# The last first-layer group accumulates onto a seed in PSUM, the second of seven products moves up, and the planner prices array-mode changes anew

## The chip, the cores and the metric

The kernel runs on one core of a Trainium2 chip. The metric is the device time of one execution in microseconds (us), the median of several runs. Engines are named as in the profile: PE (TensorE, the matrix engine), DVE (VectorE), ACT (ScalarE), POOL (GpSimd) and SP (SyncE, which here issues all DMAs).

## What is computed

Banded attention over 2 x 8 heads of 768 tokens, then two MLPs on the 1536 tokens of width 512:

```python
x = attention(q, k, v)                       # local band of 96 and 8 global keys, linear bias
h = np.maximum(x @ w_in, 0.0)                # w_in 512 x 2048
y = h * h @ w_out                            # w_out 2048 x 512: the "first layer" here
xn = y / np.sqrt(mean(y * y) + 1e-6) * rms_g
g = xn @ w_gate; val = xn @ w_val            # 512 x 1536 each: the "gated layer"
out = (g * sigmoid(g) * val) @ w_out2
```

All of it is in fp32. Each fp32 operand of the MLPs is split into a high and a low part, and a matmul becomes three: high x high, high x low, low x high (lines 334, 335, 336). Such three matmuls of 384 columns are called a triple below.

## The kernel before

Nothing is issued in the order of the source. Every operation is recorded with its engine, a modelled duration, its reads and writes and a due time; `Plan.solve` then runs a list scheduler over the model: the engine that is free first takes, of its ready operations, the one due first. Due times come from the operations that need a result, and for a triple from a running clock in the order in which the source records it. The order found is issued, and each engine executes its own list strictly in that order; a wait in the model is not a wait on the chip, and the reverse. Operations on PE have a mode: "row" (scores, line 824), "col" (probabilities times v, line 861) or "full" (all else), since they split the array differently. The model adds `MODE` = 0.095 us whenever the mode changes, and stays in the present mode if an operation of it is due within 0.25 us. While PE would idle in the first 30 us, dummy matmuls ("fillers", line 1124) are put in.

The tokens are 4 chunks (c = 0 to 3) of 384. The stages, by the time of the trace:

- Attention, 0 to 165 us: 48 tiles, chunk by chunk, each a chain of scores on PE, maximum on DVE, exponential on ACT, scaling on DVE, transposes on PE, copy on ACT and product with v on PE. Triples of the first layer for finished chunks fill PE in between.
- First layer, to 387 us: `first(g, c)` for groups g = 0 to 3 of 4 x 128 hidden columns. Its first half multiplies x by w_in into banks b4, b7, b5, b6 (groups 1 to 3); `relu2` has ACT read each bank (line 435), square it twice (436, 437) and DVE form the low part (438). Its second half multiplies the hidden values by w_out into b0 to b3, one bank for each of 4 output blocks e; group 0 copies the banks into the tile y on ACT (line 466), the later groups add them to y on DVE (line 469).
- Norm: during group 3, `norm_sum` squares y on ACT (481, 486), adds on DVE (487), sums over partitions on PE (489), takes the root on ACT (492) and the reciprocal on DVE in three pieces (495). `norm(p)`, for the pair p of chunks (2p, 2p + 1), forms the normed blocks and their differences on DVE (516, 521), the high parts on ACT and the low parts on DVE (both `split`, lines 324 and 325; results in the x tiles, or in ar).
- Gated layer, 378 to 678 us: w_gate and w_val are applied to pairs of chunks by a scheme of seven products instead of eight (`PRODUCTS`). A `quad` is one such set, six for gate and six for value per pair, each product two triples. Banks are (b1, b2, b3) = (4, 5, 6) for gate and (7, 2, 3) for value. Product 1 goes to b1 and is copied by ACT into b2 (line 551), where 6, 7 and 4 accumulate; 5 goes to b3 and ACT copies it out (554); DVE adds b2 to it after product 6 (557) and 7 (565); 2 accumulates on b1; 3 on b3. `sink` is what consumes an output. `final` multiplies by w_out2 (512 columns, lines 608 and 611).

Of the kernel before, what the change touches and what calls it, by code (L numbers as in the profile page):

```python
# [24 lines left out]
KD = DM // P  # L25
CH = 384
# [10 lines left out]
G1 = 4  # L37
N1 = FF1 // P // G1
# [12 lines left out]
QHI = KHI = "ACT"  # L51
EPS = "POOL"
NSLACK = 0.5


def f32(ap):
# [11 lines left out]
class Plan:  # L68
# [1 line left out]

    MODE = 0.095

    def __init__(self):
        self.ops = []
# [26 lines left out]
    def solve(self):  # L103
        for o in reversed(self.ops):
            for q in o.succ:
                o.due = min(o.due, q.due - o.dur - (o.lat if q.eng != o.eng else 0.0))
        engines = sorted({o.eng for o in self.ops})
        free = dict.fromkeys(engines, 0.0)
        mode = dict.fromkeys(engines)
        wait, ready = {e: [] for e in engines}, {e: [] for e in engines}  # L110
        for o in self.ops:
            o.left, o.ready = len(o.deps), 0.0
            if not o.left:
                heappush(wait[o.eng], (0.0, o.n, o))
        self.fill, done, filling, held = [], 0, True, 0.0
        while done < len(self.ops):
            best = None
            for e in engines:
                if ready[e]:
                    t = free[e]  # L120
                elif wait[e]:
                    t = max(free[e], wait[e][0][0])
                else:
                    continue
                if best is None or t < best[0]:
                    best = (t, e)
            t, e = best
            while wait[e] and wait[e][0][0] <= t:
                o = heappop(wait[e])[2]
                heappush(ready[e], (o.due, o.n, o))  # L130
            if held > t + 0.05 and any(not x[2].port for x in ready[e]):
                o = min(x for x in ready[e] if not x[2].port)[2]
                ready[e].remove((o.due, o.n, o))
                ready[e].sort()
            else:
                o = heappop(ready[e])[2]
            if o.port:
                t = max(t, held)
            if o.mode != mode[e] and len(ready[e]) and o.mode:
                other = [x for x in ready[e] if x[2].mode == mode[e] and x[0] < o.due + 0.25]  # L140
                if other:
                    heappush(ready[e], (o.due, o.n, o))
                    o = min(other)[2]
                    ready[e].remove((o.due, o.n, o))
                    ready[e].sort()
            if o is self.last_fill:
                filling = False
            if e == "PE" and t < FILL and filling:
                x = max(free[e] + 0.1, 5.0)
                while x + 0.3 < t:  # L150
                    self.fill.append(x)
                    x += 0.3
            extra = self.MODE if o.mode and mode[e] and o.mode != mode[e] else 0.0
            if o.mode:
                mode[e] = o.mode
            o.start = t
            o.end = t + o.dur + extra
            free[e] = o.end
            if o.port:
                held = o.end  # L160
            done += 1
            for q in o.succ:
                q.ready = max(q.ready, o.end + (o.lat if q.eng != e else 0.0))
                q.left -= 1
                if not q.left:
                    heappush(wait[q.eng], (q.ready + q.slack, q.n, q))
        return self
# [12 lines left out]
ACT = lambda n: 0.07 + n / 1200  # L180
# [37 lines left out]
class Mlp:  # L218
# [109 lines left out]
    def mm3(self, bank, w, a, first, last, width, rs, due=None):  # L328
        nc = self.nc

        def go():
            ps = self.tl(f"b{bank}")[:, :width]
            (wh, wl), (ah, al) = w(), a()
            nc.tensor.matmul(ps, lhsT=wh, rhs=ah, start=first, stop=False, skip_group_check=True)  # L334
            nc.tensor.matmul(ps, lhsT=wh, rhs=al, start=False, stop=False, skip_group_check=True)  # L335
            nc.tensor.matmul(ps, lhsT=wl, rhs=ah, start=False, stop=last, skip_group_check=True)  # L336
        dur = 3 * (0.0125 + width * 0.41797e-3)
        if due is None:
            due = self.clock
            self.clock += dur  # L340
        return self.op("PE", dur, go, rs, [("b", bank)], due=due, mode="full")
# [99 lines left out]
    def first(self, g, c, banks, dues=None, k_major=False):  # L441

        nc = self.nc
        b1, b2 = banks
        acts = [self.act() for _ in range(G1)]
        order = [(k, f) for f in range(G1) for k in range(KD)]
        if k_major:
            order = [(k, f) for k in range(KD) for f in range(G1 - 1)] + [(k, G1 - 1) for k in range(KD)]
        due = lambda: dues.pop(0) if dues else None
        for k, f in order:  # L450
            w, rw = self.w[("in", g * G1 + f), k]
            mm = self.mm3(b1[f], w, lambda k=k: self.x(k, c * CH, c * CH + CH), k == 0, k == KD - 1, CH,
                          rw + self.both(self.xres(k, c * CH, c * CH + CH)), due())
            if g == 0 and c == 0 and f == G1 - 1 and k == 0:
                self.plan.last_fill = mm
            if k == KD - 1:
                self.relu2(lambda f=f: self.tl(f"b{b1[f]}")[:, :CH], [("b", b1[f])], acts[f])
        order = [(e, f) for e in (0, 1) for f in range(G1 - 1)] + [(0, G1 - 1), (1, G1 - 1)]
        order += [(e, f) for e in range(2, KD) for f in range(G1)]
        for e, f in order:  # L460
            w, rw = self.w[("out", g * G1 + f), e]
            self.mm3(b2[e], w, acts[f][0], f == 0, f == G1 - 1, CH, rw + self.both(acts[f][1]), due())
            if f == G1 - 1:
                ps = lambda e=e: self.tl(f"b{b2[e]}")[:, :CH]
                if g == 0:
                    self.op("ACT", ACT(CH), lambda e=e, ps=ps: nc.scalar.copy(self.y(e, c), ps()),
                            [("b", b2[e])], self.yres(e, c))
                else:
                    self.op("DVE", DVE(CH), lambda e=e, ps=ps: nc.vector.tensor_tensor(
                        out=self.y(e, c), in0=ps(), in1=self.y(e, c), op=ALU.add),  # L470
                        [("b", b2[e])] + self.yres(e, c), self.yres(e, c))
# [3 lines left out]
    def norm_sum(self, c, bank):  # L475
# [3 lines left out]
        for e in range(KD):  # L479
# [10 lines left out]
            ps(), lhsT=self.ones, rhs=s(), start=True, stop=True, skip_group_check=True), rs, [("b", bank)],  # L490
            due=self.clock - (12.0 if bank == 7 else 0.0), mode="full", slack=NSLACK)
        self.op("ACT", ACT(CH) + 1.3, lambda: nc.scalar.activation(
# [48 lines left out]
    def quad(self, key, p, banks, sink):  # L541

        nc, tl = self.nc, self.tl
        b1, b2, b3 = banks
        ps = {b: (lambda b=b: tl(f"b{b}")[:, :CH]) for b in banks}
        n = self.np5 % 2
        self.np5 += 1
        p5, r5 = (lambda: tl(f"p5{n}")), [("p5", n)]
        rb = lambda b: [("b", b)]
        self.product(1, b1, key, p, True)  # L550
        self.op("ACT", ACT(CH), lambda: nc.scalar.copy(ps[b2](), ps[b1]()), rb(b1), rb(b2))
        yield
        self.product(5, b3, key, p, True)
        self.op("ACT", ACT(CH), lambda: nc.scalar.copy(p5(), ps[b3]()), rb(b3), r5)
        yield
        self.product(6, b2, key, p, False)
        self.op("DVE", DVE(CH), lambda: nc.vector.tensor_tensor(  # L557
            out=ps[b3](), in0=ps[b2](), in1=p5(), op=ALU.add), rb(b2) + r5, rb(b3))
        yield
        self.product(2, b1, key, p, False)  # L560
        sink(0, 0, ps[b1], rb(b1))
        yield
        self.product(7, b2, key, p, False)
        t, rt = self.ra(5)
        self.op("DVE", DVE(CH), lambda: nc.vector.tensor_tensor(
            out=t(), in0=ps[b2](), in1=p5(), op=ALU.add), rb(b2) + r5, rt)
        sink(1, 1, t, rt)
        yield
        self.product(3, b3, key, p, False)
        sink(0, 1, ps[b3], rb(b3))  # L570
        yield
        self.product(4, b2, key, p, False)
        sink(1, 0, ps[b2], rb(b2))
        yield
# [626 lines left out]
```

## Time and profile before

| | us |
|---|---|
| median of 3 runs (lowest to highest) | 676.8 (674.68 to 677.08) |
| the profiled execution, its own time | 680.09 |
| its span, first to last instruction | 678.3 |
| PE busy in the span | 653.2 |
| DVE busy | 496.6 |
| ACT busy | 387.6 |
| POOL busy | 152.2 |

The profiled execution is 3.3 us longer than the median; all times of the trace below are of it. Busy times are of matmuls whose ends are modelled and overlap, so PE at full share tells that it never waited, and not that each matmul was as short as it can be.

### The profile page before, as it was taken

What the parts mean: (1) busy time and instruction counts of PE and PEld (TensorE: products, weight loads), DVE (VectorE), ACT (ScalarE), POOL (GpSimd) and SP (SyncE); (2) the same over time, 40 slices, a digit from 0 to 9 for tenths busy, and PEclk for the clock granted to TensorE, in tenths of its full rate; (3) what the DMA queues carried; (4) which work ended last, traced back from release to release, by engine and by line L of the source; (5) the groups of instructions that cost most, each with busy time, mean ns of one, the idle gap of its engine ahead of it and who ended that gap; (6) DMA issues with size and microseconds to landing.
All of it is one profiled execution on the core that took longest, in us unless ns stands there. A gap on an engine that the chain in (4) does not pass through costs nothing. (4 is left out here: it accounts for less than half of the span.)

```text
span 678.3 us, 10579 instructions
## 1 busy us (share of the span) xinstructions
PE 653.2 (96%) x3823; PEld 592.3 (87%) x3823; DVE 496.6 (73%) x1098; ACT 387.6 (57%) x865; POOL 152.2 (22%) x187
## 2 busy tenths in 40 slices
PE   5998999998999999999999979999999999999996
PEld 4676877777999999999999968999999999998994
DVE  6989987673888966226768998877876987777434
ACT  5789878785765664346666775654353444443310
POOL 1100010002232321005300111544144234442000
PEclk9789999998999999999999988999999999999999
DMA  5435542210233323002210000131111210310022
GB/s 201 158 111 186 168 146 93 77 47 1 94 125 104 114 94 125 0 1 63 66 59 1 32 31 1 62 125 64 63 62 63 94 63 32 125 63 0 2 81 110
DMA packets 18158, 52.69 MB, mean 78 GB/s; under 512 B 2608, under 2 KB 3888, under 8 KB 18096
## 3 DMA queue, kind: packets, MB, share of 16 engines
q1 hardware_dynamic: 18096, 51.92, 23.3%
q8 instruction: 32, 0.52, 0.3%
q14 instruction: 30, 0.25, 0.1%
HBM read 48.76 MB, written 3.15 MB: 77 GB/s over the span
## 5 line engine op out<-in xcount | busy, mean ns | idle before, releaser
L325 POOL TENSOR_TENSOR M<-wbits,M 128x512 fp32r<-128x512 f32 x60 | 83.0, 1387 | 246.3 <-ACT M L324 194.6
L334 PE MATMUL b<-xh,M 128*128 128x384 f32 x336 | 117.1, 349 | 4.5 <-ACT xh L324 2.8
L335 PE MATMUL b<-xl,M 128*128 128x384 f32 x336 | 114.0, 339 | 2.0 <-DVE xl L325 2.0
L336 PE MATMUL b<-xh,M 128*128 128x384 f32 x336 | 113.8, 339 | 0.0
L438 DVE TENSOR_TENSOR h<-ra,h 128x384 fp32r<-128x384 f32 x64 | 37.3, 586 | 49.0 <-ACT ra L437 49.0
L334 PEld LDWEIGHTS b<-xh,M 128*128 128x128 f32 x336 | 64.1, 191 | 10.1 <-ACT xh L324 3.6
L335 PEld LDWEIGHTS b<-xl,M 128*128 128x128 f32 x336 | 64.0, 191 | 4.2 <-DVE xl L325 2.6
L336 PEld LDWEIGHTS b<-xh,M 128*128 128x128 f32 x336 | 63.9, 190 | 0.0
L324 ACT CAST M<-wbits 128x512 fp32r<-128x512 f32 x68 | 41.8, 617 | 37.0 <-DVE wbits L374 10.7
L334 PE MATMUL b<-h,M 128*128 128x384 f32 x176 | 61.6, 350 | 0.0
L611 DVE TENSOR_TENSOR y<-b,y 128x512 f32<-128x512 f32 x60 | 41.1, 688 | 26.2 <-PE b L336 25.8
L335 PE MATMUL b<-h,M 128*128 128x384 f32 x176 | 59.0, 335 | 0.7 <-DVE h L438 0.7
L336 PE MATMUL b<-h,M 128*128 128x384 f32 x176 | 59.0, 335 | 0.0
L435 ACT ACTIVATE ra<-b 128x384 f32<-128x384 f32 x64 | 31.2, 487 | 47.5 <-PE b L336 47.2
L366 ACT ACTIVATE wbits<-wraw 128x512 f32<-128x512 f32 x68 | 45.2, 668 | 20.7 <-DMA wraw<-in_w_in_dram 8.0
L336 PE MATMUL b<-M,h 128*128 128x512 f32 x144 | 56.9, 395 | 0.0
L335 PE MATMUL b<-M,h 128*128 128x512 f32 x144 | 56.6, 393 | 0.0
L334 PE MATMUL b<-M,h 128*128 128x512 f32 x144 | 56.2, 390 | 0.1
L371 DVE SCALAR_TENSOR_TENSOR wbits<-wraw,wbits 128x512 int32<-128x512 int32 x68 | 55.1, 811 | 1.5
L835 ACT ACTIVATE p<-p,mn 128x256 f32<-128x256 f32 (+1 forms) x96 | 46.5, 486 | 13.2 <-DVE mn L831 11.2
L374 DVE SCALAR_TENSOR_TENSOR wbits<-wraw,wbits 128x512 int32<-128x512 int32 x68 | 48.4, 714 | 0.9
L839 POOL TENSOR_SCALAR rs<-sm 128x2 f32<-128x2 f32 x48 | 12.7, 265 | 143.4 <-ACT p L835 143.4
(124 smaller groups left out, 1598.6 us busy)
## 6 DMA issues: line engine op xcount, KB each, us to landing
wraw<-in_w_out_dram SPq DMA_DIRECT2D x28, 512.0 KB, 3.5
wraw<-in_w_in_dram SPq DMA_DIRECT2D x16, 512.0 KB, 3.5
wraw<-in_w_gate_dram SPq DMA_DIRECT2D x12, 512.0 KB, 3.5
wraw<-in_w_val_dram SPq DMA_DIRECT2D x12, 512.0 KB, 3.5
raw<-in_kq_dram SPq DMA_DIRECT2D x8, 480.0 KB, 3.5
v<-in_vab_dram SPq DMA_DIRECT2D x8, 384.0 KB, 3.0
out_dram<-y SPq DMA_DIRECT2D x12, 256.0 KB, 2.1
raw<-in_kq_dram SPq DMA_DIRECT2D x7, 416.0 KB, 3.4
```

Of the source, the lines that this page charges most:

```text
L324: self.op("ACT", ACT(n), lambda: nc.scalar.copy(dst()[0], src()), rs, [(x, "hi") for x in ws])
L325: self.op(eng, t(n), lambda: e.tensor_tensor(out=dst()[1], in0=src(), in1=f32(dst()[0]), op=ALU.subtract), rs + [(x, "hi") for x in ws], [ ...
L334: nc.tensor.matmul(ps, lhsT=wh, rhs=ah, start=first, stop=False, skip_group_check=True)
L335: nc.tensor.matmul(ps, lhsT=wh, rhs=al, start=False, stop=False, skip_group_check=True)
L336: nc.tensor.matmul(ps, lhsT=wl, rhs=ah, start=False, stop=last, skip_group_check=True)
L366: self.plan.add("ACT", ACT(512), lambda: nc.scalar.activation(tl(bits), f32(tl(raw)[:, :, 1]), AF.Abs), rr, rb)
L371: self.plan.add("DVE", DVE(512), lambda: v.scalar_tensor_tensor(out=bi(), in0=tl(raw)[:, :, 0], scalar=29, in1=bi(), op0=ALU.logical_shift ...
L374: self.plan.add("DVE", DVE(512), lambda: v.scalar_tensor_tensor(out=bi(), in0=tl(raw)[:, :, 1], scalar=-(1 << 30), in1=bi(), op0=ALU.bitwi ...
L435: self.op("ACT", ACT(CH), lambda: nc.scalar.activation(t(), src(), AF.Relu), rsrc, rt)
L438: self.op("DVE", DVE(CH), lambda: nc.vector.tensor_tensor(out=get()[1], in0=t(), in1=f32(get()[0]), op=ALU.subtract), rt + hi, lo, port=True)
L611: self.op("DVE", DVE(DM), lambda tok=tok, ps=ps: nc.vector.tensor_tensor(out=self.o(tok), in0=ps(), in1=self.o(tok), op=ALU.add), [("b", b ...
L835: self.op("ACT", 0.29 + w / 1200, lambda j=j: nc.scalar.activation(tl(f"p{m}")[:, j, :w], tl(f"p{m}")[:, j, :w], AF.Exp, bias=tl(f"mn{m}") ...
```

## The change

Three edits. In group 3 of the first layer, for every chunk, ACT first copies the block of y into its bank ("seed"), the triples accumulate onto it without clearing the bank, and ACT copies the sum back to y; the DVE add of line 469 no longer occurs for this group. In `quad`, product 2 and its sink are recorded next after product 1, ahead of 5 and 6. In the planner, a change of mode into "full" costs 0.085 us more in the model, and where a full operation would be next and none of the present mode is due within 0.25 us, a row or col operation that is ready and due within 1.0 us is taken first.

```diff
+NEAR = 1.0
...
-    MODE = 0.095
+    MODE, BACK = 0.095, 0.085
...
+                if not other and o.mode == "full":
+                    other = [x for x in ready[e] if x[2].mode and x[2].mode != "full" and x[0] < o.due + NEAR]
...
-            extra = self.MODE if o.mode and mode[e] and o.mode != mode[e] else 0.0
+            extra = 0.0
+            if o.mode and mode[e] and o.mode != mode[e]:
+                extra = self.MODE + (self.BACK if o.mode == "full" else 0.0)
...
+        seed = g == N1 - 1
+        if seed:
+            for e in range(KD):
+                self.op("ACT", ACT(CH), lambda e=e: nc.scalar.copy(self.tl(f"b{b2[e]}")[:, :CH], self.y(e, c)),
+                        self.yres(e, c), [("b", b2[e])])
...
-            self.mm3(b2[e], w, acts[f][0], f == 0, f == G1 - 1, CH, rw + self.both(acts[f][1]), due())
+            self.mm3(b2[e], w, acts[f][0], f == 0 and not seed, f == G1 - 1, CH, rw + self.both(acts[f][1]), due())
...
-                if g == 0:
+                if g == 0 or seed:
...
+        self.product(2, b1, key, p, False)
+        sink(0, 0, ps[b1], rb(b1))
+        yield
         self.product(5, b3, key, p, True)
...
-        yield
-        self.product(2, b1, key, p, False)
-        sink(0, 0, ps[b1], rb(b1))
```

What this does to the orders is seen best at three places. In the rows below a name is followed by its buffer and a number of the build; the lines of the changed kernel are 5 to 13 higher (324 is 329, 334 to 336 are 339 to 341, 435 is 440, 466 for the copy to y is 476 and the seed is 466, 557 is 570).

The first place is ACT's list in group 3, while the first half of chunk 3 runs on PE: the splits of `norm(0)` and then the first relu of chunk 3. Before:

```order
L324 CAST xh0_337<-nq2_3288 128x384
L324 CAST xh1_426<-nq3_3408 128x384
L324 CAST ar_1882<-nq1_3266 128x384
L324 CAST ar_1882<-nq0_3250 128x384
L324 CAST xh1_426<-nq2_3288 128x384
L324 CAST ar_1882<-nq3_3408 128x384
L324 CAST xh2_516<-nq1_3266 128x384
L435 ACTIVATE ra0_664<-b4_1875 128x384
```

and in the changed kernel, from the same place on:

```order
L476 COPY y1_85<-b0_492 128x384
L329 CAST ar_1884<-nq1_3268 128x384
L329 CAST ar_1884<-nq0_3247 128x384
L476 COPY y1_85<-b1_530 128x384
L476 COPY y1_85<-b2_538 128x384
L466 COPY b0_492<-y1_85 128x384
L329 CAST xh1_425<-nq2_3292 128x384
L466 COPY b1_530<-y1_85 128x384
L329 CAST ar_1884<-nq3_3415 128x384
L329 CAST xh2_527<-nq1_3268 128x384
L476 COPY y1_85<-b3_142 128x384
L466 COPY b2_538<-y1_85 128x384
```

Four copies of chunk 2's sums to y and three seeds of chunk 3 now stand among the same splits; the first relu of chunk 3 follows, and the fourth seed stands between it and the relu of b5. The relu of b6 has all eight ahead of it.

The second place is DVE's list around the three reciprocals of chunk 3's norm, at the start of `norm(1)`. Before:

```order
L516 SCALAR_TENSOR_TENSOR nq1_3266<-y1_85,gcol_61,ns0_3239 128x384
...
L325 TENSOR_TENSOR xl0_338<-nq1_3266,xh0_337 128x384
L374 SCALAR_TENSOR_TENSOR wbits2_402<-wraw1_182,wbits2_402 128x512
L557 TENSOR_TENSOR b3_142<-b2_576,p51_3788 128x384
L495 RECIPROCAL ns1_3403<-ns1_3403 128x128 x3
L516 SCALAR_TENSOR_TENSOR nq0_3250<-y1_85,gcol_61,ns1_3403 128x384
L521 TENSOR_TENSOR nq2_3288<-nq0_3250,nq1_3266 128x384
```

and in the changed kernel, the start and the end of the stretch (18 rows of `norm(1)` lie between):

```order
L379 SCALAR_TENSOR_TENSOR wbits2_385<-wraw1_182,wbits2_385 128x512
L505 RECIPROCAL ns1_3408<-ns1_3408 128x128 x3
L526 SCALAR_TENSOR_TENSOR nq0_3247<-y1_85,gcol_61,ns1_3408 128x384
L531 TENSOR_TENSOR nq2_3292<-nq0_3247,nq1_3268 128x384
L330 TENSOR_TENSOR xl0_331<-nq1_3268,xh0_330 128x384
...
L330 TENSOR_TENSOR xl2_528<-nq2_3292,xh2_527 128x384
L570 TENSOR_TENSOR b3_142<-b2_538,p51_3797 128x384
```

The low part xl0 of chunk 2's block moved from before the reciprocals to after them, and the add of line 557 (now 570), which frees b2 for product 7 of the value quad of pair 0, moved from before them to 22 operations behind them. The low part xl2 of chunk 2's next block is the 13th operation behind the reciprocals before, and the 18th now.

The third place is PE's list after the partition sum of line 489 (499), first matmul of each triple. Before:

```order
L489 MATMUL b1_536<-ns1_3403,ones_59 128x384
...
L334 MATMUL b4_1875<-xh0_337,M3_640 128x384
...
L334 MATMUL b2_576<-ar_1882,M8_2477 128x384
...
L334 MATMUL b3_142<-xh1_426,M8_2477 128x384
...
L334 MATMUL b6_1916<-xh0_337,M4_699 128x384
...
L334 MATMUL b4_1875<-xh2_516,M3_640 128x384
```

and now:

```order
L499 MATMUL b1_530<-ns1_3408,ones_59 128x384
...
L339 MATMUL b4_1877<-xh0_330,M3_579 128x384
...
L339 MATMUL b6_1918<-xh0_330,M4_676 128x384
...
L339 MATMUL b4_1877<-xh2_527,M3_579 128x384
...
L339 MATMUL b4_1877<-xh1_425,M3_579 128x384
...
L339 MATMUL b6_1918<-xh2_527,M4_676 128x384
...
L339 MATMUL b2_538<-ar_1884,M8_2479 128x384
```

Between the last triple of the first layer and the partition sum stand 13 triples before and 8 now, and between that and the first triple of pair 1 (b4 from xh0) 5 before and 10 now. The four triples with M8 (products 7 and 3 of the value quad of pair 0) stood behind the first triple of pair 1 and stand now behind its fifth. From group 2 to the end of the first layer PE's list is the same in both kernels. In the attention stage the list is rearranged in many places; it has 180 changes of mode before and 183 now, and 23 fillers before and 25 now.

## Rows read from the trace of the kernel before

**Rows 1.** Windows by stage: busy us (x instructions), granted clock, DMA.

```profile
40.00:100.00 60.00, 57.43 (x449) 44.72 (x447) 56.33 (x185) 51.16 (x139) 5.18 (x17) 1.00 0.54 171
400.00:414.00 14.00, 8.60 (x25) 6.28 (x24) 13.69 (x28) 7.81 (x16) 0.00 (x0) 0.63 0.00 0
414.00:660.00 246.00, 246.00 (x1288) 228.92 (x1287) 178.75 (x311) 108.87 (x219) 83.80 (x77) 1.00 0.19 62
```

**Rows 2.** PE's waits, 376 to 410 us: total us, times, longest.

```profile
PE b L334 <- ACT xh L324: 2.8, 2, 1.6
PE b L335 <- DVE xl L325: 2.0, 2, 1.2
PE b L334 <- ACT b L551: 0.6, 1, 0.6
PE b L334 <- ACT ra L435: 0.5, 1, 0.5
```

**Rows 3.** PE's waits, 413.8 us to the end: all of them.

```profile
PE b L334 <- DVE ra L565: 0.7, 1, 0.7
```

**Rows 4.** PE in order of time, 376 to 409 us: start, duration, line, [idle before].

```profile
377.31 0.45 PE L334 MATMUL b<-xh,M 128*128 128x384 f32 x1 [0.46 <-ACT ra L435]
...
386.99 0.33 PE L334 MATMUL b<-h,M 128*128 128x384 f32 x1
...
387.51 0.33 PE L334 MATMUL b<-ar,M 128*128 128x384 f32 x1
...
394.27 0.81 PE L489 MATMUL b<-ns,ones 128*128 128x384 f32 x2
...
399.60 0.33 PE L334 MATMUL b<-xh,M 128*128 128x384 f32 x1
...
401.56 0.44 PE L334 MATMUL b<-xh,M 128*128 128x384 f32 x1 [1.28 <-ACT xh L324]
...
408.59 0.69 PE L334 MATMUL b<-ar,M 128*128 128x384 f32 x1 [0.61 <-ACT b L551]
```

**Rows 5.** ACT in order of time, 376 to 397 us.

```profile
376.79 0.47 ACT L435 ACTIVATE ra<-b 128x384 f32<-128x384 f32 x1
...
394.87 1.28 ACT L492 ACT_TABLE_LOAD   x1
396.17 0.58 ACT L492 ACTIVATE ns<-b,epst 128x384 f32<-128x384 f32 x1
```

**Rows 6.** DVE in order of time, 371 to 407 us.

```profile
371.49 1.94 DVE L469 TENSOR_TENSOR y<-b,y 128x384 f32<-128x384 f32 x4
...
397.15 2.56 DVE L495 RECIPROCAL ns<-ns 128x128 f32<-128x128 f32 x3
399.75 0.62 DVE L516 SCALAR_TENSOR_TENSOR nq<-y,gcol,ns 128x384 f32<-128x384 f32 x1
...
406.37 1.02 DVE L325 TENSOR_TENSOR xl<-nq,xh 128x384 fp32r<-128x384 f32 x2
```

**Rows 7.** Windows: two at half clock, one of ACT before chunk 3's relus.

```profile
24.60:38.30 13.70, 13.70 (x73) 9.19 (x69) 11.02 (x43) 8.64 (x27) 1.50 (x4) 0.50 0.37 127
364.00:376.80 12.80, 12.80 (x75) 12.53 (x73) 12.63 (x27) 9.61 (x22) 1.30 (x1) 1.00 0.00 0
403.50:413.70 10.20, 7.27 (x20) 5.49 (x19) 10.03 (x21) 5.46 (x12) 0.00 (x0) 0.50 0.00 0
```

**Rows 8.** Groups by line: count, busy us, mean ns of one, idle before.

```profile
L436 ACT ACTIVATE h<-ra 128x384 fp32r<-128x384 f32 x64 | 33.6, 525 | 1.8
L466 ACT COPY y<-b 128x384 f32<-128x384 f32 x16 | 7.4, 474 | 3.5 <-PE b L336 3.2
L469 DVE TENSOR_TENSOR y<-b,y 128x384 f32<-128x384 f32 x48 | 25.5, 550 | 15.1 <-PE b L336 14.9
```

**Rows 9.** PE in attention: a triple's first matmuls right behind scores.

```profile
101.46 0.44 PE L334 MATMUL b<-h,M 128*128 128x384 f32 x1
101.74 0.34 PE L335 MATMUL b<-h,M 128*128 128x384 f32 x1
101.92 0.34 PE L336 MATMUL b<-h,M 128*128 128x384 f32 x1
```

## The prediction

> **What bounds the kernel now.** I read the windows by stage first, then PE's waits in the stages that the change touches, then PE, DVE and ACT in order of time where PE waits.
>
> The windows [rows 1] divide the run into three kinds of stretch. Between 40 and 100 us DVE is busy for 56.3 of 60 us and PE for 57.4: the two bound it together. From 414 to 660 us PE is busy for all 246 us at full clock, and from 413.8 us to the end its waits amount to one of 0.7 us [rows 3]. Whatever is taken from DVE or ACT there is worth nothing; an edit can only lose. Between 400 and 414 us PE is busy for 8.6 of 14 us and DVE for 13.7: that is the hole of this kernel, and DVE is what it waits for. PE's waits there [rows 2] are for high and low parts made by `norm(1)` (2.8 and 2.0 us) and for one copy of line 551 (0.6).
>
> In order of time [rows 4]: the last triple of the first layer ends at 387.51, from here on called T. A triple takes 0.52 us (386.99 to 387.51). The partition sum for chunk 3 stands at 394.27, PE runs out of work after the triple of 399.60, that is at 400.1 = T + 12.6, and after 408.59 = T + 21.1 it waits no more. Between these two it executes three triples, so 8.5 - 3 x 0.52 = 6.9 us are lost. The granted clock then stands at half from 403.5 to 413.7 [rows 7], so the triples from 408.59 to 413.7 take twice their time, some 2.6 us more. The hole costs about 9.5 us in all; that is the most that the relief of DVE could give back.
>
> The path into the hole: the root of chunk 3 ends at 396.17 + 0.58 = T + 9.2 [rows 5], the three reciprocals run from 397.15 to 399.7, and the low part xl2, which PE needs before it runs on, starts at 406.37, twelve operations behind 399.75 [rows 6]. That is 0.55 us for each operation of `norm(1)`.
>
> **The seeds: what they remove and add.** Removed are 16 DVE adds of 0.55 us [rows 8], 8.8 us. Added are 16 seeds and 16 copies on ACT. A copy out of the bank is line 466's, 0.47 us; a copy from SBUF into PSUM is not in this trace. Its nearest rows are that 0.47 (out of PSUM) and 0.53 (SBUF to SBUF, line 436) [rows 8]; I take 0.47, the nearer form. ACT gains 15 us, DVE loses 8.8 us, and the triples are the same in number. Only where one of the two engines sets PE's time does it matter.
>
> It matters first before chunk 3's relus. The four adds of chunk 2 at 371.49 [rows 6] go, and eight copies of 3.8 us come into ACT's list ahead of the relu of b6. Before the change this relu runs at 376.79 [rows 5], and the triple on b6 waits for it until 377.31 [rows 4]. From 364.0 to 376.8 ACT is busy 9.6 of 12.8 us [rows 7]; with every idle moment filled, 3.8 - 3.2 = 0.6 us would be added, with none filled 3.8. Walking the list of the changed kernel with these durations, most of the idle time stands before splits that DVE feeds and some of it cannot be filled; I get the relu 1.3 us later. Behind it stand PE's triple and with it all that follows. **+1.3 us** (0 to 3.8; nothing, if DVE's lead of 1.9 us from the four adds brings the splits forward).
>
> **The hole, with the new order.** Let T' be the new T. On PE the partition sum stands 8 triples behind T', at T' + 4.2, not 6.8. Chunk 3's last copy, square and add (0.47 + 0.53 + 0.55, behind one another and behind the bank's last triple) are done by T' + 2.6, so it need not wait. On ACT stand then a table load and an activation, line 366, a cast, the copies 551 and 554, where 554 waits for a triple that ends at T' + 4.2, then the second table load and the root: 4.2 + 0.2 + 0.5 + 0.5 + 1.3 + 0.6, about T' + 7.4. Reciprocals: T' + 7.5 to T' + 10.1. Before they ended at T + 12.2, so the chain starts 2.1 us earlier. That is the gain of the edit.
>
> The order spends it. xl2 is the 18th operation behind the reciprocals and not the 13th: 17 x 0.55 = 9.4, plus its own 0.5, so T' + 20.0 against T + 19.4. xl2 for PE's fifth triple of pair 1 is the 22nd: T' + 22.2. The first triple of pair 1, which before ran without a wait behind 5 others, now waits for xl0, 2 operations and its own 0.5 behind the reciprocals: T' + 11.7. And the add of line 557 stands behind the 22nd, so the four triples with M8, which before filled 2.1 us of PE, can't be there to fill. PE: 18 triples and the sum until T' + 10.4; then first triple at 11.7, second at 14.0, third at 20.1, fourth and fifth by T' + 22.8, and from there on without waiting. Lost between 10.4 and 22.3: 11.9 - 4 x 0.52 = 9.8 us, against 6.9 + 0.5 of short waits inside triples (7.4). **+2.4 us**. The stretch at half clock I take to be as costly as before, since PE is idle as long; it is 2.6 us either way, within 1.5 us.
>
> From below: if DVE runs `norm(1)` at 0.48 us per operation (the four adds of rows 6 show 1.94 / 4), the 22 operations end 1.5 us earlier, and with a root at T' + 6.5 another 0.9: then the hole is the same as before. From above: a half-clock stretch that lasts 4 us longer, +2 us.
>
> A table load holds ACT for 1.28 us and the root starts 0.02 us behind it [rows 5]. The Trainium skill ("ScalarE: Activation LUTs", section "What ACT_TABLE_LOAD costs") counts a drain of 1.38 us on top at each switch; the trace doesn't show one. By the page the two loads in the chain would put the end of the hole 2.8 us later still.
>
> **The seven products.** Product 2 now has to follow product 1 on the same bank behind ACT's copy of it. In the order of the changed kernel at least three triples (1.55 us) stand between them in steady state, and the copy needs about 0.47 + 0.2. The other side of it: 7 follows 6, with DVE's add of line 557 between, at three triples where four or more stood before; the add takes 0.55 + 0.25, which leaves 0.7 us for whatever DVE has ahead of it, and DVE is busy 178.8 of 246 us there. Before, no such place waited. No gain is possible (PE has no wait to give back). Between nothing and 0.3 us at each of ten pairs, I take **+0.6 us** (0 to 3).
>
> **The planner.** Mode changes rise from 180 to 183. Behind scores the step from a triple's first matmul to the second is 0.28 us, to the third 0.18 [rows 9], so a change back costs 0.10 us: +0.3 us. Two fillers more stand in the stretch at half clock from 24.6 to 38.3 us [rows 7], where PE is busy throughout: 2 x 0.32. Against it, more work on PE there may end that stretch earlier. Between 40 and 100 us DVE holds the pace and its work is the same. **+0.3 us** (-3 to +2).
>
> **Sum.** 1.3 + 2.4 + 0.6 + 0.3 = +4.6 us on the profiled execution's 680.1: 684.7. It stands 3.3 us over the median of 676.8; on the median the forecast is 681.4. What a measurement here can tell from no change is about 0.5%, 3.4 us.
>
> **The rivals.**
>
> No change. The copies fit into ACT's idle time, DVE runs `norm(1)` at 0.48 us, and the hole is as long as before, with the products at nothing: -1 to +3 us, 676 to 680. For it: each of these is an end of a bound above. Against it: the four M8 triples are missing from the hole whatever DVE's pace.
>
> Faster. Relief of DVE reaches PE: the adds of chunks 2 and 3 (4.4 us) are gone ahead of the reciprocals, and the root of chunk 3 comes as early as ACT's list allows. If PE's last wait ends by T' + 18 rather than T' + 22.3, PE loses 18 - 10.4 - 2.1 = 5.5 us and not 7.4, and if the half-clock stretch then shrinks with it, up to 2.6 more are gained: with the other terms at nothing 672 to 675. It decides whether the 22nd operation behind the reciprocals ends before T' + 18. For it: DVE is busy 13.7 of 14 us in the hole, so what frees DVE should show there first [rows 1]. Against it: 22 operations at the shortest step seen, 0.48 us, take 10.6 us behind a root at T' + 7.4 and 2.6 us of reciprocals.
>
> Slower still. DVE's add of line 557 is late in most pairs and PE waits 0.3 to 0.5 us some twenty times in the gated layer, or the table loads drain as the page has it: 685 to 690.
>
> **How the numbers follow.** Forecast (slower by 3.4 to 7 us) 0.42; slower still 0.10; no change 0.27; faster 0.21. The time is that of the likeliest, 681.4, its own range 679 to 684. The range to hold 8 in 10 goes to 672.5 on the side of the faster case and to 688 on the other, by the bounds -3 for the planner, the hole's -2.4 and +2, the relus' 0 to 3.8 and the products' +3. Slower by over 0.5%: 0.52; within: 0.27; faster: 0.21.
>
> **What would show it.** In the profile of the changed kernel: PE waits for the relu of b6 about 1.8 us, not 0.5; DVE no longer shows the adds in group 3; the reciprocals of chunk 3 start some 7.5 us behind the last triple of the first layer; PE waits for xl2 longest, over 5 us, and resumes 22 us behind that triple; the gated layer shows waits for lines 557 and 565 or none. It is wrong if PE resumes before T' + 20, if the attention stage ends more than 2 us earlier (now about 165 us), or if the half-clock stretches change in number.

## The result and the profile after

| | before | after |
|---|---|---|
| median of 6 runs, us | 676.94 (674.68 to 680.45) | 681.55 (680.73 to 682.83) |
| the profiled execution, its own time, us | 680.09 | 680.73 |

The changed kernel is slower: its time is 1.0055 times that of before, with a 95% interval of 1.0032 to 1.0078. The two profiled executions differ by only 0.64 us. Why they are closer than the medians matters for the reading, so it comes first.

Windows of the changed kernel: the stretch that ran at half clock before, the stretch up to the relu of b6 (as long as that of [rows 7]), the hole, and the stretch at half clock in it (the granted clock is the column behind POOL's):

```profile
24.60:38.30 13.70, 12.64 (x101) 8.50 (x100) 13.13 (x51) 11.07 (x33) 1.79 (x5) 1.00 0.48 136
360.80:373.60 12.80, 12.80 (x75) 12.64 (x73) 12.59 (x24) 12.32 (x29) 1.56 (x1) 1.00 0.00 0
400.00:414.00 14.00, 10.09 (x38) 9.18 (x39) 12.63 (x25) 7.02 (x15) 1.56 (x1) 0.63 0.01 2
400.40:410.60 10.20, 6.69 (x19) 5.78 (x20) 9.19 (x20) 4.75 (x10) 0.00 (x0) 0.50 0.00 0
```

The stretch at half clock of [rows 7] at 24.6 us is not there, and 101 matmuls ran in it, not 73. So the last triple of the first layer ends at T' = 384.28 and not at T = 387.51, and 3.2 us of what is lost later are hidden in the comparison of the two profiles. A second profile of the kernel before (first experiment) has its T at 385.12, so most of this is a matter of the execution and not of the change. So all profiles are compared below from T on, by the start of the last matmul: 288.36 us behind T in the changed kernel (672.64 - 384.28), 284.38 before (671.89 - 387.51). That is 4.0 us more; the medians differ by 4.6.

PE's waits from 380 to 410 us, and from 410 us to the end:

```profile
PE b L340 <- DVE xl L330: 4.3, 3, 1.6
PE b L339 <- ACT xh L329: 3.0, 1, 3.0
PE b L339 <- ACT b L561: 0.6, 1, 0.6
```

```profile
PE b L339 <- DVE y L621: 0.9, 3, 0.3
PE b L339 <- DVE ra L575: 0.7, 1, 0.7
```

Before, these sums were 5.4 [rows 2, without the relu] and 0.7 [rows 3]. The hole has grown, and the gated layer has three waits that it had not: for the final add of line 621 (611 before). PE in order of time, first at the relu of b6, then in the hole:

```profile
374.16 0.45 PE L339 MATMUL b<-xh,M 128*128 128x384 f32 x1 [0.40 <-ACT ra L440]
374.44 0.34 PE L340 MATMUL b<-xl,M 128*128 128x384 f32 x1
374.62 0.33 PE L341 MATMUL b<-xh,M 128*128 128x384 f32 x1
...
384.28 0.33 PE L339 MATMUL b<-xh,M 128*128 128x384 f32 x1
...
388.44 0.81 PE L499 MATMUL b<-ns,ones 128*128 128x384 f32 x2
...
394.29 0.34 PE L339 MATMUL b<-xh,M 128*128 128x384 f32 x1
396.23 0.44 PE L340 MATMUL b<-xl,M 128*128 128x384 f32 x1 [1.60 <-DVE xl L330]
...
398.41 0.44 PE L340 MATMUL b<-xl,M 128*128 128x384 f32 x1 [1.40 <-DVE xl L330]
...
402.01 0.69 PE L339 MATMUL b<-xh,M 128*128 128x384 f32 x1 [2.98 <-ACT xh L329]
404.00 0.69 PE L340 MATMUL b<-xl,M 128*128 128x384 f32 x1 [1.29 <-DVE xl L330]
...
405.61 0.69 PE L339 MATMUL b<-xh,M 128*128 128x384 f32 x1 [0.61 <-ACT b L561]
```

and the two engines it waits for there, ACT and DVE:

```profile
389.60 1.28 ACT L502 ACT_TABLE_LOAD   x1
390.89 0.58 ACT L502 ACTIVATE ns<-b,epst 128x384 f32<-128x384 f32 x1
```

```profile
391.89 2.56 DVE L505 RECIPROCAL ns<-ns 128x128 f32<-128x128 f32 x3
394.49 0.62 DVE L526 SCALAR_TENSOR_TENSOR nq<-y,gcol,ns 128x384 f32<-128x384 f32 x1
...
403.39 0.55 DVE L330 TENSOR_TENSOR xl<-nq,xh 128x384 fp32r<-128x384 f32 x1
...
406.04 0.56 DVE L570 TENSOR_TENSOR b<-b,p 128x384 f32<-128x384 f32 x1
```

The chain starts as early as it should (reciprocals at T' + 7.6; they started at 397.15 = T + 9.6 before [rows 6]) and PE resumes no sooner all the same (T' + 21.3 against T + 21.1 [rows 4]), with less done: PE is through with what needs nothing of the late norm at 394.29 = T' + 10.0, over two microseconds sooner than before (T + 12.6). The add of line 570 that lets the four M8 triples start is at 406.04, behind everything.

### The profile page after: what moved, and what is told of

Same layout as the page of the kernel before. It is cut to its first block, busy times and chain, and to the rows that moved or that the text cites. A ratio compares the mean times of both kernels' runs of the same rounds, so it can differ in the third digit from the quotient of the medians.

```text
span 678.9 us, 10594 instructions
## 1 busy us (share of the span) xinstructions
PE 649.3 (96%) x3825; PEld 587.9 (87%) x3825; DVE 499.7 (74%) x1082; ACT 401.3 (59%) x897; POOL 152.6 (22%) x187
## 4 chain that ended last, share of the span: by engine, by line
PE 75%; DVE 20%; ACT 3%; issue 1%; DMA 0%; DVEq 0%; ACTq 0%
PE b L339 23%; PE b L341 22%; PE b L340 22%; DVE wbits L376 2%; PE ps L834 2%; DVE p L841 2%; PE av L871 2%; PE tb L862 2%; DVE p L855 2%; DVE wbits L374 1%; DVE wbits L379 1%; DVE wbits L372 1%; DVE xl L330 1%; DVE ra L597 1%; DVE y L621 1%
## 5 line engine op out<-in xcount | busy, mean ns | idle before, releaser
L376 DVE SCALAR_TENSOR_TENSOR wbits<-wraw,wbits 128x512 int32<-128x512 int32 x68 | 61.3, 902 | 1.6
L621 DVE TENSOR_TENSOR y<-b,y 128x512 f32<-128x512 f32 x60 | 41.1, 687 | 21.6 <-PE b L341 20.9
L379 DVE SCALAR_TENSOR_TENSOR wbits<-wraw,wbits 128x512 int32<-128x512 int32 x68 | 51.4, 756 | 0.8
```

The lines of the kernel that those rows point to most:

```text
L376: self.plan.add("DVE", DVE(512), lambda: v.scalar_tensor_tensor(out=bi(), in0=tl(raw)[:, :, 0], scalar=29, in1=bi(), op0=ALU.logical_shift ...
L379: self.plan.add("DVE", DVE(512), lambda: v.scalar_tensor_tensor(out=bi(), in0=tl(raw)[:, :, 1], scalar=-(1 << 30), in1=bi(), op0=ALU.bitwi ...
L621: self.op("DVE", DVE(DM), lambda tok=tok, ps=ps: nc.vector.tensor_tensor(out=self.o(tok), in0=ps(), in1=self.o(tok), op=ALU.add), [("b", b ...
```

## The experiments

### Each edit alone, and the kernel before once more

The planner's part, the seeds and the move of product 2 were each put on the kernel before by themselves:

```diff
+                    other = [x for x in ready[e] if x[2].mode and x[2].mode != "full" and x[0] < o.due + NEAR]
...
+                extra = self.MODE + (self.BACK if o.mode == "full" else 0.0)
```

> The planner's two new rules on the kernel before, no seeds, old order of the products. Theory (the order of the products loses the time, in the hole and in the gated layer): PE's list behind the attention is that of the kernel before, so the time is within 1.5 us of the kernel before (677), and the hole ends at T + 21. Rival A (the rearranged attention loses it): 680 or more, attention ends 2 us later or a half-clock stretch lasts longer.

```diff
+        seed = g == N1 - 1
...
+                if g == 0 or seed:
```

> The seeds on the kernel before, old planner, old order of the products. In its list the add that frees b2 for product 7 stands 17 operations behind the reciprocals (22 in the changed kernel, ahead of them before) and xl2 14 (18 and 13). Theory (order of the products): reciprocals end at T + 10.2, add of b2 at T + 19.3, PE runs on at about T + 19.3 to 19.8; loss in the hole 7.0 to 7.5 us, as before; no waits for the final add in the gated layer; 676 to 678. Rival B (the seeds lose it: they delay the reciprocals' root and the relus, or push the add of b2 behind the reciprocals): 680 or more.

```diff
+        self.product(2, b1, key, p, False)
+        sink(0, 0, ps[b1], rb(b1))
+        yield
         self.product(5, b3, key, p, True)
```

> The new order of the products on the kernel before, no seeds, old planner. xl2 is the 17th operation behind the reciprocals, the add that frees b2 the 22nd, and the four triples with M8 stand behind it. Theory: PE runs dry at T + 12.3 and runs on at T + 23 to 24, so the hole costs 2 to 3 us more than before; waits for the final add in the gated layer cost 1 to 1.5 us: 680 to 681.5. Rival B (the seeds lose it): 677. Rival A (the planner): 677.

The kernel before, unchanged:

> The kernel before once more, for its profile. If the half-clock stretch of 3.4 us that the first profile shows at 164.6 us is a matter of one execution, it is absent here, attention ends 1.5 to 2 us earlier and the profiled time is near 677; if it belongs to the kernel's order, it is there again and the profiled time is near 680.

| | median, us | ratio to before (95%) | T, us | start of the last matmul | behind T |
|---|---|---|---|---|---|
| before, first profile | 676.94 | | 387.51 | 671.89 | 284.38 |
| before, second profile | one run, 678.08 | | 385.12 | 669.90 | 284.78 |
| planner alone | 678.37 | 1.0014 (0.9994 to 1.0035) | 384.47 | 668.64 | 284.17 |
| seeds alone | 677.13 | 0.9986 (0.9961 to 1.0011) | 384.54 | 668.46 | 283.92 |
| products alone | 680.30 | 1.0044 (1.0026 to 1.0062) | 384.48 | 671.93 | 287.45 |
| all three | 681.55 | 1.0055 (1.0032 to 1.0078) | 384.28 | 672.64 | 288.36 |

Here and below each ratio is to runs of the kernel before that took turns with the kernel in question (their medians are 677.65 in this experiment, 677.19 and 678.10 in later ones), so it is not the quotient of two medians of the table.

The second profile of the kernel before, two windows:

```profile
24.60:38.30 13.70, 12.64 (x101) 8.63 (x101) 13.23 (x50) 11.70 (x37) 3.04 (x5) 1.00 0.48 147
60.60:67.40 6.80, 6.56 (x24) 5.67 (x24) 5.69 (x16) 4.77 (x13) 0.00 (x0) 0.50 0.43 140
```

The same program has its half-clock stretch at another place and a shorter one, and the stretch of 3.4 us at 164.6 us that the first profile shows is absent here, as I expected of a matter of one execution. So T moves by 2.4 us between two executions of one kernel, and the column behind T is the one to read. By it the move of product 2 loses 2.9 us (against the mean of the two profiles of before, 284.6), the planner -0.4 and the seeds -0.7; all three lose 3.8. (Behind the attention the planner alone has the list of the kernel before, so its -0.4 tells how far two executions of one list lie apart.) The medians say the same: only the products are slower than before by more than the measurement is uncertain. The rivals that blame the seeds or the planner are out. The three parts add up to 1.8 us, and not 3.8. In these profiles the move of product 2 is dearer beside the seeds, and the rows place it in the hole: PE runs dry at T + 11.0 and its last wait ends at T + 20.8 with the products alone, at T' + 10.0 and T' + 21.3 with all three, 1.5 us more from the one to the other. The medians do not show it (1.0044 and 1.0055, with intervals that overlap), and no run has the seeds and the move without the planner.

Where it goes shows in PE's count of matmuls in the 22 us behind T, one row each for before (second profile), seeds alone, products alone, and the changed kernel:

```profile
385.12:407.12 22.00, 16.45 (x81) 14.38 (x81) 20.89 (x36) 14.82 (x26) 5.34 (x5) 0.88 0.07 24
```

```profile
384.54:406.54 22.00, 16.83 (x75) 14.51 (x75) 21.39 (x37) 15.93 (x29) 4.86 (x5) 0.80 0.07 24
```

```profile
384.48:406.48 22.00, 14.57 (x71) 12.69 (x71) 20.59 (x39) 15.45 (x28) 5.67 (x6) 0.85 0.07 24
```

```profile
384.28:406.28 22.00, 14.12 (x68) 11.99 (x68) 21.44 (x36) 16.14 (x30) 4.92 (x5) 0.87 0.07 24
```

With the seeds alone the reciprocals come earlier and PE's last wait ends at T + 19.0 rather than T + 21.1, but it also runs dry two microseconds earlier: the hole moves forward and keeps its length. The gain on DVE was real and bought nothing that stands out of the spread. With the products alone the last wait ends at T + 20.8 (I had expected 23 to 24: an operation of the norm takes less than 0.55 us) and ten matmuls fewer are done 22 us behind T. They also show the three waits for the final add (line 611 here, three times, 0.9 us of idle time in all), so those belong to this edit.

### Which part of the new order loses

In one kernel the first of the six blocks of gated columns has the old order of the products, the other five the new one (`old` puts product 2 and its sink behind product 6 again):

```diff
+        old = key[1] == 0
+        if not old:
+            self.product(2, b1, key, p, False)
...
+        if old:
+            self.product(2, b1, key, p, False)
```

> The changed kernel with the old order of the products in the first of the six blocks of gated columns alone (both pairs), the new order in the other five. DVE's list behind the reciprocals is then that of the seeds alone: the add that frees b2 stands 17 behind, not 23, and the four triples with M8 stand ahead of product 2 of pair 1. Theory (the new order loses 1.5 to 2 us in the hole by what it puts ahead there, and 1.4 us by three waits for the final add later): PE runs on at T + 19, the three waits remain, 678 to 679.5. Rival (the new order loses a little at every pair): 680.5 or more. Rival (all of it is the hole): 677.

It took 679.18 us, 1.0025 times before (1.0007 to 1.0043), and from T to the last matmul 285.03 us: 3.3 less than the changed kernel, 1.1 more than the seeds alone. In the 22 us behind T it is the seeds alone again:

```profile
387.23:409.23 22.00, 16.84 (x75) 14.52 (x75) 21.40 (x37) 15.93 (x29) 4.88 (x5) 0.79 0.07 24
```

and of the waits for the final add two are left, where I had expected three (this kernel's line 627):

```profile
PE b L339 <- DVE y L627: 0.6, 2, 0.3
```

So the hole's loss comes from the order in the first block; which of its two pairs was not tried apart. By the lists it is this: product 2 of pair 1, recorded earlier, is due earlier; its triples, and the DVE operations that make their operands out of chunk 3's norm, come ahead of the add and the four M8 triples of pair 0, which need nothing of that norm. The other 1.1 us are mostly the two waits, 0.9 by the steps below.

The second kernel asks what these waits are. Around the first of the three, DVE, POOL and PE of the changed kernel, each in order of time:

```profile
528.94 1.78 DVE L376 SCALAR_TENSOR_TENSOR wbits<-wraw,wbits 128x512 int32<-128x512 int32 x1
530.64 0.68 DVE L621 TENSOR_TENSOR y<-b,y 128x512 f32<-128x512 f32 x1
```

```profile
528.64 1.53 POOL L330 TENSOR_TENSOR M<-wbits,M 128x512 fp32r<-128x512 f32 x1 [6.65 <-ACT M L329]
```

```profile
530.74 0.34 PE L341 MATMUL b<-xh,M 128*128 128x384 f32 x1
531.37 0.50 PE L339 MATMUL b<-M,h 128*128 128x512 f32 x1 [0.29 <-DVE y L621]
```

Line 376 prepares weight bits and takes 0.69 us as a rule (the median of its 68). Here POOL makes the low part of a weight tile at the same time, and line 376 ends at 530.72, 0.55 us behind POOL's end at 530.17. The final add behind it is late, and PE with it: 0.63 us from one start to the next, where 0.17 does without the wait (531.86 to 532.03 in the kernel that follows). In this experiment that POOL operation is left out in the last five blocks, and with it the low part of that tile; nothing else differs in any list:

```diff
-        self.op(eng, t(n), lambda: e.tensor_tensor(
+        self.op(eng, t(n), lambda: skip or e.tensor_tensor(
...
-                self.block((kind, 2 * g + f), slot, LOG)
+                self.block((kind, 2 * g + f), slot, LOG, skip=f == 0 and g > 0)
```

> The changed kernel without one POOL operation in each of the last five blocks: the low part of the first w_out2 tile is not computed (the old contents of its buffer are used). The lists of PE, DVE and ACT are the same. Theory (DVE's weight operation of line 376, whose operands are all in SBUF, is held until the POOL operation beside it ends, 1.78 us where it takes 0.69 elsewhere, and the final add behind it is late): at the three places line 376 takes 0.69 us, PE's waits for the final add (3 x 0.47 us) are gone, 680.1 us, 1.4 less than the changed kernel. Rival (the add is late because the list puts three weight operations ahead of it): the waits stay, 681.5.

It took 680.17 us (1.0029 of before, 1.0007 to 1.0052), and 286.80 us from T to the last matmul (672.15 - 385.35), 1.56 less than the changed kernel. DVE and PE at the same place:

```profile
530.05 0.68 DVE L376 SCALAR_TENSOR_TENSOR wbits<-wraw,wbits 128x512 int32<-128x512 int32 x1
530.66 0.68 DVE L621 TENSOR_TENSOR y<-b,y 128x512 f32<-128x512 f32 x1
```

```profile
531.86 0.34 PE L341 MATMUL b<-xh,M 128*128 128x384 f32 x1
...
532.03 0.40 PE L339 MATMUL b<-M,h 128*128 128x512 f32 x1
```

Line 376 takes 0.68 us, and all three waits are gone. So the list alone does not make them. Nor does the meeting with POOL alone: in the kernel before, this line (371) meets POOL too, with up to 1.73 us behind 414 us, and no final add is waited for. It takes the meeting and the new list together. By the medians alone this would not be decided, since the two intervals overlap; the rows decide.

The Trainium skill ("GPSIMD Engine Reference", section "Specifications") says that GpSimd shares its SBUF interfaces with VectorE and contends with DVE instructions that run in a two-port performance mode or have two SBUF inputs. The trace agrees: line 376 reads two tiles of SBUF, while line 621, which reads one of its inputs from PSUM, is not held by a POOL operation that runs beside it from 469.36 to 470.88 (first row). Two SBUF inputs are not needed for it: line 374, which has one, took 1.40 us beside POOL where it takes 0.43 as a rule (last two rows); no view here shows in which mode it ran.

```profile
469.67 0.69 DVE L621 TENSOR_TENSOR y<-b,y 128x512 f32<-128x512 f32 x1
...
613.22 1.53 POOL L330 TENSOR_TENSOR M<-wbits,M 128x512 fp32r<-128x512 f32 x1 [0.64 <-ACT M L329]
613.64 1.40 DVE L374 TENSOR_SCALAR wbits<-wbits 128x512 int32<-128x512 int32 x1
```

### Filling the hole

If the hole is a row of DVE operations that only independent triples can fill, the cure is to have more of these. `norm(1)` mixes blocks of chunk 2 (B11, B21), which need no reciprocal of chunk 3, with blocks that do. Here the four blocks of chunk 2 go first, with two buffers more:

```diff
-        for n in range(4):
+        for n in range(6):
             tl.define(f"nq{n}", late, [P, CH], F32)
...
+        def early(q, fin, diff, part):
+            fin("B11"), part("B11"), fin("B21"), part("B21")
...
+        def late(q, fin, diff, part):
+            fin("B12"), diff("T1", "B12", "B11"), fin("B22"), part("T1"), diff("T3", "B22", "B12"), part("B22"), part("T3")
+            diff("T2", "B22", "T1"), part("T2"), diff("T4", "B21", "T2"), part("T4")
...
+                slot = {"B11": x, "T1": x, "T2": x, "B21": z, "T4": z, "B12": 0, "T3": 0, "B22": 3}
...
+        for x in todo:
+            early(*x)
+        for x in todo:
+            late(*x)
```

It was put on the seeds alone, on the changed kernel, on the kernel before, and on the products alone:

> The seeds, old planner, old order of the products, and the norm of the second pair in two halves: first the four blocks of chunk 2 alone (B11 and B21), which need no reciprocal of chunk 3, then the rest (two more buffers for normed blocks). Theory (the hole is the row of DVE operations behind the reciprocals, filled only by triples that need none of them): xl2 of chunk 2 stands ahead of the reciprocals, the add that frees b2 5 behind them and not 17, the four M8 triples and two more run early; the hole loses 2 to 4 us and not 7.2, 671 to 674. Rival (DVE is the bound there: what is moved ahead of the reciprocals makes them as much later, 8 x 0.55 = 4.4 us): 676 to 678.

> The changed kernel (all three edits) with the norm of the second pair in the same two halves. In its list product 2 of pair 1 and product 1 of its value quad need nothing of chunk 3, so that ten triples (5.2 us) can run in the hole. Theory: the hole loses 1.5 to 3 us and the half-clock stretch gets shorter or goes; with three waits of 0.47 us in the gated layer left, 671 to 674, as good as or better than the seeds alone with it. Rival (DVE bound): 679 to 682.

> The kernel before with the norm of the second pair in two halves alone; none of the three edits. Its list has the add that frees b2 ahead of the reciprocals and xl2 of chunk 2 too; behind the sum stand 12 triples that need nothing of chunk 3. Theory (what counts in the hole is how many triples need nothing of the reciprocals, not when these start): PE runs dry at T + 17 and not T + 12.6, the hole loses 2 to 4 us, the half-clock stretch goes, 671 to 674; the seeds are worth nothing beside it. Rival (the seeds make the room on DVE that the split needs): 676 or more.

> The kernel before with the new order of the products and the norm of the second pair in two halves; no seeds, old planner. Its list behind the reciprocals is, but for the seeds, that of all three edits with the split. Theory: the new order of the products, which lost 3 us alone, loses nothing here, since product 2 of pair 1 needs nothing of chunk 3 any more: within 1.5 us of the split on the kernel before, 671 to 674. Rival (the new order loses by itself): 3 us over the split on the kernel before.

| split norm on | median, us | ratio to before (95%) | T, us | start of the last matmul | behind T | PE's waits, us | half clock, us |
|---|---|---|---|---|---|---|---|
| the kernel before | 673.94 | 0.9944 (0.9922 to 0.9965) | 385.61 | 667.03 | 281.42 | 4.0 | 6.8 |
| seeds | 674.15 | 0.9949 (0.9930 to 0.9968) | 387.65 | 668.30 | 280.65 | 5.4 | none |
| products | 675.44 | 0.9951 (0.9932 to 0.9970) | 385.78 | 667.59 | 281.81 | 3.6 | 3.4 |
| all three edits | 673.46 | 0.9938 (0.9914 to 0.9962) | 385.56 | 665.27 | 279.71 | 3.0 | none |

All four beat both kernels, and their intervals overlap. The last two columns are of the hole: the sum of PE's waits from 376 to 412 us, without the one for the relu, and the length of the stretch at half clock. Without the split the waits sum to 5.4 us before, 5.2 with the seeds, 7.4 with the products and 7.9 with all three, each with 10.2 us at half clock.

With all three edits, the window of 22 us behind T, the one of 400 to 414 us, and PE's waits from 380 to 412 us are:

```profile
385.56:407.56 22.00, 19.00 (x102) 17.24 (x101) 20.92 (x36) 16.49 (x31) 3.62 (x3) 1.00 0.00 1
400.00:414.00 14.00, 12.89 (x65) 11.34 (x66) 13.93 (x30) 7.74 (x17) 0.00 (x0) 1.00 0.01 2
```

```profile
PE b L339 <- DVE b L588: 1.2, 1, 1.2
PE b L339 <- ACT b L579: 1.0, 1, 1.0
PE b L340 <- DVE xl L330: 0.4, 1, 0.4
PE b L339 <- DVE ra L593: 0.4, 1, 0.4
```

102 matmuls instead of 68 in the same 22 us, PE's waits 3.0 us instead of 7.9, and no stretch at half clock, though the reciprocals start 1.7 us later (394.83, that is T + 9.3). The rival that DVE is simply full there is out: it is as busy as before (20.9 of 22 us), and only the order of its work is another.

Filled waits are not the whole of it. On the seeds they did not shrink at all (5.4 us, where the seeds alone have 5.2; I had expected the loss to halve); what went there is the half-clock stretch, and 3.3 us behind T with it. PE's waits there from 380 to 412 us, now apart from each other (they end at 393.35, 403.06 and 407.30), and its clock:

```profile
PE b L334 <- DVE b L580: 2.6, 1, 2.6
PE b L334 <- ACT b L574: 1.4, 1, 1.4
PE b L334 <- DVE ra L588: 1.4, 1, 1.4
```

```profile
400.00:414.00 14.00, 10.08 (x56) 9.29 (x56) 13.76 (x29) 6.29 (x13) 0.00 (x0) 1.00 0.01 2
```

On the kernel before, where I had expected the stretch to go, it only got shorter:

```profile
402.40:409.20 6.80, 5.45 (x18) 4.94 (x17) 6.66 (x15) 3.00 (x7) 0.00 (x0) 0.50 0.00 0
```

So the gain is in part filled waits and in part clock, in shares that differ from kernel to kernel, and why one keeps the full clock and another not stays open.

The move of product 2, which lost 2.9 us on the kernel before, loses nothing beyond the uncertainty here (281.81 against 281.42 behind T). That is a balance: 200 matmuls behind T the split with the move is 1.4 us ahead (42.74 against 44.10), since product 2 of pair 1 then needs nothing of chunk 3 and fills the hole, and two waits that only it has (for DVE's lines 578 and 325, at 470 and 478 us) take that back. With the seeds beside it the time behind T is the shortest of all. By the medians the four can't be told apart, so that the seeds and the new order are worth something here stays unproven.

## Why the prediction was right

The forecast of 681.4 us and slower was met (681.55), and the term that decided, the hole, came near to what was worked out. Two of the smaller terms were wrong, one in each direction, so that the sum agrees to 0.2 us is in part luck.

**Seeds.** The price of a copy was right: 0.474 us out of the bank as taken, and 0.482 into it, which the trace before had not shown:

```profile
L476 ACT COPY y<-b 128x384 f32<-128x384 f32 x32 | 15.0, 474 | 10.2 <-PE b L341 10.1
L466 ACT COPY b<-y 128x384 f32<-128x384 f32 x16 | 7.5, 482 | 2.0 <-DVE y L479 1.9
```

The 8.8 us that DVE was to lose are not in its total: it is busy 496.6 us before, 495.3 with the seeds alone and 499.7 in the changed kernel. There the 16 adds are gone, but lines 376 and 379 take 112.7 us together where 371 and 374 took 103.5.

**The relu of b6, +1.3 us, was mis-sized: it was nothing.** PE waits 0.40 us for it (374.16), 0.46 before [rows 4], and not 1.8. The 600 matmuls ahead of T, the same in both lists, take 105.57 us, and 105.72 and 105.74 in the two profiles of before; with the seeds alone 105.58. The step that failed is "some of it cannot be filled": from 360.8 to 373.6 us ACT was busy 12.3 of 12.8 us in the changed kernel, against 9.6 of 12.8 [rows 7]. The lower end of my range named a possible reason, that DVE, freed of four adds, brings the splits forward; that this is why was not tried apart.

**The hole, +2.4 us, was right in its mechanism and near in size.** Sum at T' + 4.2 (4.2 predicted), reciprocals at T' + 7.6 (7.5), PE dry at T' + 10.0 (10.4), first triple at T' + 11.9 (11.7), second at 14.1 (14.0), third at 19.7 (20.1), PE on for good at 21.3 (22.3). The last microsecond is the 0.55 us per operation, which was 0.52 from 394.49 to 403.39. Of the 4.0 us that the profile loses behind T, 1.4 are the three later waits, and 2.6 remain; against the second profile of before 2.2. Counted behind the hole alone, where the 201st matmul behind T starts, it is 2.2 and 1.9 (49.31 us, against 47.10 and 47.46). I put the loss to the new order behind the reciprocals, and the runs sharpen this: it is the move of product 2, not the seeds, that puts the M8 triples behind. The longest wait was not for xl2, as I wrote, but for ACT's high part xh of the same block (2.98 us at 402.01); xl2 then adds 1.29. It is one chain, and I had priced its end. The half-clock stretch in the hole was as long as before, as I took it: it lasts from 400.4 to 410.6 us. The root starts 0.01 us behind its table load (389.60 + 1.28). The Trainium skill ("ScalarE: Activation LUTs", section "What ACT_TABLE_LOAD costs") counts a drain on top; this trace shows none either.

**The seven products, +0.6 us, were mis-sized and for another reason.** They cost 1.4 us (3 x 0.46). I looked at the waits inside a quad, at lines 557 and 565; these stayed as they were. What came was a wait for the final add, which stands behind a weight operation that POOL holds up; the lists do not show that.

**The planner, +0.3 us, can't be told from nothing** (1.0014, 0.9994 to 1.0035). Nor do [rows 9] single out the mode as what costs 0.10 us: the same two steps, 0.28 and 0.18 us, follow the wait at 374.16 us in the changed kernel, where the mode does not change.

So the sum was +4.6 and the profiles behind T say +3.6 to +4.0: 1.3 too much in the relus, 0.8 too little in the products. One test that I had named was badly chosen: a change in the number of the half-clock stretches would make the prediction wrong. They did change between the two profiles (two fewer), and so they do between two executions of the kernel before. The test beside it, that attention ends more than 2 us earlier, was not met: its last matmul ends at 163.6 us before and at 162.0 in the changed kernel.

## What to carry to other kernels

When an engine's work is taken off the path into a wait, ask what fills the wait: an earlier start with as little independent work behind it only moves the idle time forward. Look for work whose inputs are ready before the late value and have it listed first; here this gave 0.5 to 0.6%, part of it by a shorter stretch at half clock, where the three edits lost about as much. And compare profiles from a common event behind which the kernels differ, not by their ends.

## What the runs showed of the hardware

A DVE operation with two SBUF inputs that starts beside a running POOL tensor operation was held to POOL's end: in the changed kernel all 15 such starts of line 376 end 0.55 us behind the POOL operation and take 0.98 to 1.78 us instead of 0.69. Line 374, with one SBUF input, was held as well (1.40 us instead of 0.43), but a reciprocal with one was not (line 495 at 397.15 us in the kernel before, 0.94 us as elsewhere). Line 621, with one input in PSUM, took 0.68 to 0.69 us in all 17 such cases. The three places where PE felt it cost 1.4 us.

The half-clock stretches of TensorE in and just behind the attention stage belong to the execution: 24.6 to 38.3 us and 164.6 to 168.0 us in one profile of the kernel before, 60.6 to 67.4 us in the other, none in the changed kernel's. The one in the hole is 10.2 or 10.3 us long in all eight profiles without the split norm, and 6.8, 3.4, 0 and 0 us with it. The sum of PE's idle time does not decide it: with the split on the seeds PE idles 5.4 us in three places and there is none, with the split on the kernel before it idles 4.0 us and there are 6.8 us.
